# A second Strassen level for product 4 of batches 3 to 6 with its sums on GpSimd, and x transposed in blocks of two tokens of one head

## The chip, the cores and the metric

The kernel runs on one core of a Trainium2 chip. A core has five engines with a queue each: TensorE (PE; its weight loads are listed apart, as PEld), VectorE (DVE), ScalarE (ACT), GpSimd (POOL) and SyncE (SP, which here only issues transfers). Each queue is worked in order; an instruction that waits for another engine holds back everything behind it on its own engine. The metric is the device time of one execution in microseconds. The kernel before took 201.92 us (median of three runs, 201.89 to 202.7).

## The reference

Per batch (8) and head (8), x has 512 tokens of 64 values and the state 32 rows of 64.

```python
a  = softmax(x @ state.T / 8);   xread = a @ state     # 512 x 64 per head
a2 = softmax(state @ x.T / 8);   sread = a2 @ x        #  32 x 64 per head
attn = concat([xread, sread], axis=2)                  # 544 rows per batch, 512 wide
h = attn @ w_in                                        # 512 -> 2048
out = (0.5 * h * (1 + erf(h / sqrt(2)))) @ w_out       # 2048 -> 512
```

The inputs and the output (4352 x 512) are float32; the kernel computes in bfloat16 with float32 sums.

## The kernel before, in words

**First matrix product.** For the 512 read rows of a batch, w_in is multiplied into the state first: `p_mm` forms P = state · w_in, so that h = a · P. `scores` forms x · state^T and its exponential `e`; `norm` (DVE) makes `a`; a DMA transpose (`atr_dma`) makes `AT`. `M(i)` (`mm1`) is one 128-row block of h^T, two matmuls of 512 columns (L506) with a gelu on ACT that writes `g` (L513). There are 16 such blocks per batch.

**Second matrix product.** g^T · w_out (512 x 2048 by 2048 x 512) is done by Strassen's scheme in Winograd's form: seven products of quadrants, named "1" to "7". Products 1, 2 and 4 take a quadrant of g as it is; 5, 6, 7 and 3 take sums of quadrants that DVE forms (`g_sum`, tile `gsum`). The right sides are quadrants of w_out or differences of them (`w_diff`, tiles `ws`). A product is 16 matmuls of 256 columns (L647) into one bank; `X(b, name)` runs it and hands the bank to ACT (`snap`, a copy to SBUF) or to DVE (an add into the output tile `oh`). `c4`, the copy of product 4, is used by `c21`, the add into the left half of the second output tile, after product 7 of the same batch.

**The second level.** Product 2 of batches 2 to 7 is already split again into seven small products of four matmuls with 128 columns each (`sub_mm`, L727). `sub_sums` makes the four left sums on DVE (`gsub`). `sub_a` runs 2, 1, 4, 5 into the four quarters of the bank, and ACT copies the bank to `qa` (L741). `sub_b` adds 6 and 3 and restarts quarter 0 with 7 in that same bank, ACT copies it to `qb` (L749), and three adds on DVE make `c2`. The pools `cpool` give one buffer per tag.

**Order.** The order is written out by hand. A batch b has eight slots p = 0 to 7. Each holds two blocks `M` of batch b; slots 0 to 5 hold products 1, 6, 5, 7 and 3 of batch b-1, the scores of batch b+1 (slot 1), its norm (slots 2 and 3) and its `p_mm` (slot 5, `p_all`). Slot 5 ends with `sub_a`, slot 6 with `sub_b`, slot 7 with product 4 of batch b. The last batch's slots 0 to 4 interleave the rows of sread (`read_out_slot`).

**x.** POOL issues the load of x (with a cast) into `xb`, where a partition holds four tokens of every head. `rearr` (POOL) makes a copy `x4` in which the blocks of 128 columns pair two heads, and `xtr_dma` (SP) transposes these blocks to `xT` by DMA; batch 1 is transposed on PE (`xtr`, L271). `rearr_ones` (POOL) makes `xo`, the copy with a column of ones for sread. `sbd` holds the transposed states, block-diagonal for the two heads of a block; `state_prep` (L160, L166) fills it with one PE transpose per batch. `hold_for` is a one-element POOL copy that delays the next load until a given gelu.

The change and the prediction's steps touch `state_prep`, `xtr`, `xtr_dma`, `scores`, `rearr`, `w_subs`, `sub_sums`, `sub_a`, `sub_b` and the order of the loop.

Of the kernel before, what the change touches and what calls it, by code (L numbers as in the profile page):

```python
# [17 lines left out]
def kernel(  # L18
# [8 lines left out]
    nc = tc.nc  # L27
# [41 lines left out]
    sbd = persist.tile([128, B, HC, 2 * NS], BF16, name="sbd")  # L69
# [7 lines left out]
    sb0 = persist.tile([128, 2, 2, 2, NS], BF16, name="sb0")  # L77
    hold = persist.tile([128, 1], BF16, name="hold")
    spare = persist.tile([128, 1], FP32, name="spare")
    warm = persist.tile([128, 512], BF16, name="warm")  # L80
    xos = [persist.tile([128, SJ, HC, 132], BF16, name=f"xo_{i}") for i in range(2)]
    x4s = [persist.tile([128, SJ, HC, 128], BF16, name=f"x4_{i}") for i in range(2)]
# [12 lines left out]
    nc.gpsimd.memset(sbd, 0.0)  # L95
# [38 lines left out]
    def load_rest():  # L134
        load_w_out(4, 6)
        load_w_out(6, 8)
        load_w_in(1024, 1536)
        load_w_out(8, 12)
        load_w_in(1536, 2048)
        load_st(2, 3)  # L140
        load_x(2)
        load_w_out(12, 16)
        load_x(3)

# [10 lines left out]

    def state_prep(b0, b1, pool=ps_f, tag="f"):
        n = b1 - b0
        ps = pool.tile([128, n, HC, NS], BF16, name="st_ps", tag=tag)
        for b in range(b0, b1):
            nc.tensor.transpose(  # L160
                ps[:, b - b0, :, :].rearrange("p c n -> p (c n)"),
                st_bf[:, b, :, :].rearrange("q t d -> q (t d)"),
                ident,
            )
        for t in range(2):
            nc.vector.tensor_copy(  # L166
                out=sbd[64 * t:64 * t + 64, b0:b1, :, 32 * t:32 * t + 32].rearrange(
                    "d b c n -> d (b c) n"
                ),
                in_=ps[64 * t:64 * t + 64, :, :, :].rearrange("d b c n -> d (b c) n"),  # L170
            )
# [23 lines left out]
    def state0_p(ps):  # L195
        for t in range(2):
            h = slice(64 * t, 64 * t + 64)
            nc.scalar.copy(out=sbd[h, 0, :, 32 * t:32 * t + 32], in_=ps[h, 2, :, :])
# [7 lines left out]
    def begin(b):  # L206
        A = Att()
        atts[b] = A
        A.x4 = x4s[b % 2]
        A.xo = xos[b % 2]  # L210
        if b > 0:
            A.xT = att.tile([128, SJ, HC, 128], BF16, name="xT", tag="xT")
# [7 lines left out]

    def rearr(b, ts=(0, 1)):
        A = atts[b]
        src = xbs[b].rearrange("p (t c) (j d) -> p t c j d", t=2, d=D)
        for t in ts:
            nc.gpsimd.tensor_copy(  # L225
                out=A.x4[:, :, :, 64 * t:64 * t + 64].rearrange("p j c d -> p c j d"),
                in_=src[:, t],
            )
# [35 lines left out]
    def xtr(b, cs):  # L264
        A = atts[b]
        xv = xbs[b].rearrange("p (t c) (j d) -> p j c t d", t=2, d=D)
        ps = ps_f.tile([128, len(cs), SJ, 128], BF16, name="xT_ps", tag="f")
        for i, c in enumerate(cs):
            for j in range(SJ):
                for t in range(2):  # L270
                    nc.tensor.transpose(ps[64 * t:64 * t + 64, i, j, :], xv[:, j, c, t, :], ident)  # L271
        nc.vector.tensor_copy(
            out=A.xT[:, :, cs[0]:cs[0] + len(cs), :].rearrange("p j c n -> p c j n"), in_=ps
        )

    def xtr_dma(b):
        A = atts[b]
        nc.sync.dma_start_transpose(
            out=A.xT.rearrange("p j c n -> p (j c) n"),
            in_=A.x4.rearrange("p j c n -> p (j c n)"),  # L280
# [44 lines left out]
    def scores(b, half):  # L325
# [4 lines left out]
        for ci in range(2):  # L330
            c = 2 * half + ci
            for j in range(SJ):
                nc.tensor.matmul(  # L333
                    pt[:, j, :, ci, :],
                    lhsT=A.xT[:, j, c, :],
                    rhs=sbd[:, b, c, :],
                    start=True,
                    stop=True,
                )
# [95 lines left out]
    def p_mm(b, f, tiles):  # L435
# [3 lines left out]
        for c in range(HC):  # L439
            for t in range(2):  # L440
                nc.tensor.matmul(  # L441
                    ps[t][32 * c:32 * c + 32, :],
                    lhsT=sbd[64 * t:64 * t + 64, b, c, 32 * t:32 * t + 32],
# [36 lines left out]
    def pmat00(h):  # L480
# [3 lines left out]
        for c in range(HC):  # L484
            for t in range(2):
                nc.tensor.matmul(
                    ps[t][32 * c:32 * c + 32, :],
                    lhsT=sbd[64 * t:64 * t + 64, 0, c, 32 * t:32 * t + 32],
# [868 lines left out]
```

## Time and profile before

| what | us |
|---|---|
| median of three runs | 201.92 |
| the profiled execution | 202.25 |
| its span (first to last instruction) | 200.3 |
| PE busy | 193.9 (97%) |
| DVE busy | 155.1 (77%) |
| ACT busy | 145.6 (73%) |
| POOL busy | 48.1 (24%) |

The profiled execution is 1.95 us longer than its span: that lies ahead of the first and behind the last instruction shown. The granted TensorE clock is full in all 40 slices. A busy share is an average over the whole span; whether an engine is late in one place is read from the timeline there. In the timeline a line holds the start, the time from start to the end of the last instruction of the group, the engine, line, operation, tiles and count, and in brackets idle time and what ended it. Matmuls follow each other faster than each ends (one of 512 columns every 0.22 us, though each is listed with 0.38), so the time that a group costs PE is the distance to the start of the next group.

### The profile page before, as it was taken

How to read it: one execution, taken by the hardware profiler on the slowest of the kernel's cores; microseconds unless marked ns; L12 is line 12 of the kernel's file. 1: busy time of each engine (PE TensorE's matmuls, PEld its weight loads, DVE VectorE, ACT ScalarE, POOL GpSimd, SP SyncE). 2: the span in 40 equal slices, each digit the busy share in tenths (PEclk: the TensorE clock that was granted, in tenths of full speed). 3: DMA queues.
4: the chain of work that ended last, by engine and by line, in shares of the span. 5: the costliest groups of instructions: out<-in, count | busy, mean ns of one | idle time of the engine just before them, and what ended most of it. 6: DMA issues, size and time to landing. Idle time of an engine off the chain costs nothing.

```text
span 200.3 us, 5055 instructions
## 1 busy us (share of the span) xinstructions
PE 193.9 (97%) x2102; PEld 134.3 (67%) x2107; DVE 155.1 (77%) x279; ACT 145.6 (73%) x264; POOL 48.1 (24%) x65
## 2 busy tenths in 40 slices
PE   7899999999999999999999999999999999999993
PEld 2533544465767777767777787677776888878893
DVE  2963796969989769975997798849966897984863
ACT  3785577699896799569966997599948778775120
POOL 8972504543403444040504300030000000000000
PEclk9999999999999999999999999999999999999999
DMA  5999999976494959680797025420024010030044
GB/s 192 197 174 202 206 199 201 183 136 142 84 149 77 241 65 164 141 214 0 77 188 209 5 67 95 138 75 27 28 107 106 0 55 0 7 153 0 18 146 157
DMA packets 40567, 23.16 MB, mean 116 GB/s; under 512 B 21856, under 2 KB 39136, under 8 KB 40544
## 3 DMA queue, kind: packets, MB, share of 16 engines
q0 software_dynamic: 13984, 8.10, 29.9%
q1 hardware_dynamic: 25728, 14.22, 27.5%
q10 hardware_dynamic: 832, 0.52, 0.8%
q8 instruction: 16, 0.26, 0.5%
q14 instruction: 7, 0.06, 0.1%
HBM read 17.30 MB, written 8.91 MB: 131 GB/s over the span
## 4 chain that ended last, share of the span: by engine, by line
PE 86%; DMA 5%; POOL 4%; ACT 2%; issue 0%; DVE 0%; POOLq 0%
PE xp L647 36%; PE hp L506 26%; DMA xb<-in_x_dram 5%; PE xp L727 5%; PE op L548 3%; PE sp L866 3%; PE rp L932 3%; POOL w_in_bf L105 2%; PE op L532 2%; PE xp L773 2%; PE pt L333 2%; ACT P L1002 1%; PE p_ps L441 1%; PE sr L962 1%; POOL sbd L95 1%; POOL w_out_bf L113 1%
## 5 line engine op out<-in xcount | busy, mean ns | idle before, releaser
L513 ACT ACTIVATE g<-hp 128x512 bf16<-128x512 f32 x124 | 67.1, 614 | 17.0 <-PE hp L506 16.8
L506 PE MATMUL hp<-AT,P 128*128 128x512 bf16 x248 | 62.2, 379 | 0.0
L647 PEld LDWEIGHTS <-gsum 128*128 128x128 bf16 x416 | 40.4, 98 | 8.9 <-issue 0.4
L647 PE MATMUL xp<-ws,gsum 128*128 128x256 bf16 x320 | 38.2, 273 | 0.0
L506 PEld LDWEIGHTS <-P 128*128 128x128 bf16 x248 | 23.0, 98 | 19.4 <-ACT P L452 0.7
L647 PEld LDWEIGHTS <-g 128*128 128x128 bf16 x240 | 23.3, 98 | 4.8
L637 DVE TENSOR_TENSOR gsum<-g 128x2048 bf16<-128x2048 bf16 x14 | 17.0, 1218 | 0.6 <-ACT g L513 0.6
L225 POOL COPY x<-xb 128x1024 bf16<-128x1024 bf16 x12 | 12.2, 1044 | 18.5 <-DMA xb<-in_x_dram 18.5
L235 POOL COPY xo<-xb 128x1024 bf16<-128x1024 bf16 x12 | 12.2, 1043 | 14.1 <-PE sr L962 13.9
L647 PE MATMUL xp<-w_out_bf,g 128*128 128x256 bf16 x128 | 15.3, 273 | 0.0
L647 PE MATMUL xp<-ws,g 128*128 128x256 bf16 x112 | 13.4, 273 | 0.0
L1016 POOL COPY hold<-g 128x1 bf16<-128x1 bf16 x7 | 2.3, 334 | 42.9 <-ACT g L513 42.9
L666 DVE TENSOR_TENSOR c<-qb 128x256 f32<-128x256 f32 x6 | 2.6, 425 | 12.7 <-ACT qb L749 12.7
L548 PE MATMUL op<-w_out_bf,g 128*128 128x512 bf16 x44 | 11.0, 380 | 0.5 <-issue 0.3
L647 PE MATMUL xp<-w_out_bf,gsum 128*128 128x256 bf16 x96 | 11.5, 273 | 0.0
L666 DVE TENSOR_TENSOR oh<-xp,c 128x512 f32<-128x512 f32 x14 | 9.6, 686 | 2.4 <-PE xp L647 2.0
L1002 DVE CAST P<-p_ps 128x512 bf16<-128x512 f32 x15 | 9.4, 683 | 2.4 <-PE p_ps L441 2.4
L356 DVE TENSOR_TENSOR a<-e,ics 128x512 bf16<-128x512 bf16 x14 | 10.5, 750 | 0.5
L353 DVE TENSOR_REDUCE cs<-e 128x16 f32<-128x512 bf16 x14 | 9.5, 678 | 0.9 <-ACT e L340 0.9
L513 ACT ACT_TABLE_LOAD x7 | 9.0, 1283 | 0.1
L441 PE MATMUL p_ps<-w_in_bf,sbd 64*32 64x512 bf16 x248 | 9.0, 380 | 0.0
L637 DVE TENSOR_TENSOR gsum<-gsum,g 128x2048 bf16<-128x2048 bf16 x7 | 8.6, 1225 | 0.2
(155 smaller groups left out, 308.9 us busy)
## 6 DMA issues: line engine op xcount, KB each, us to landing
out_dram<-oh SPq DMA_DIRECT2D x15, 256.0 KB, 3.3
xb<-in_x_dram POOLq DMA_DIRECT2D x7, 512.0 KB, 7.1
out_dram<-oh SPq DMA_DIRECT2D x6, 512.0 KB, 3.1
w_in_bf<-in_moe_w_in_dram POOLq DMA_DIRECT2D x6, 256.0 KB, 11.7
out_dram<-osb SPq DMA_DIRECT2D x5, 256.0 KB, 3.0
w_out_bf<-in_moe_w_out_dram POOLq DMA_DIRECT2D x4, 256.0 KB, 7.8
w_out_bf<-in_moe_w_out_dram POOLq DMA_DIRECT2D x2, 512.0 KB, 13.3
x0f<-in_x_dram SPq DMA_DIRECT2D x3, 256.0 KB, 3.8
```

What stands on the lines that cost most here:

```text
L225: nc.gpsimd.tensor_copy(out=A.x4[:, :, :, 64 * t:64 * t + 64].rearrange("p j c d -> p c j d"), in_=src[:, t],)
L235: eng.tensor_copy(out=A.xo[:, :, :, 2 + 64 * t:66 + 64 * t].rearrange("p j c d -> p c j d"), in_=src[:, t],)
L356: nc.vector.tensor_tensor(out=A.a[:, :, hs].rearrange("p g (c n) -> p g c n", n=NS), in0=e4, in1=ics[:, :, :].to_broadcast((128, G, 2, NS) ...
L441: nc.tensor.matmul(ps[t][32 * c:32 * c + 32, :], lhsT=sbd[64 * t:64 * t + 64, b, c, 32 * t:32 * t + 32], rhs=w_in_bf[64 * t:64 * t + 64, c ...
L506: nc.tensor.matmul(hp, lhsT=Ps[b][:, t, m * 128:(m + 1) * 128], rhs=atts[b].AT[:, :, t, :], start=(t == 0), stop=(t == 1),)
L513: nc.scalar.activation(out=gs[b][:, m, :], in_=hp, func=AF.Gelu)
L548: nc.tensor.matmul(ops[b, j], lhsT=gs[b][:, m, j * 128:(j + 1) * 128], rhs=w_out_bf[:, m, :], start=(m == 0), stop=(m == MC - 1),)
L637: nc.vector.tensor_tensor(out=got[name], in0=x, in1=y, op=op)
L647: nc.tensor.matmul(ps[:, j - js[0], :], lhsT=lhs[:, m, 128 * j:128 * j + 128], rhs=rhs[:, m, :], start=(first and j == js[0] and m == 0), ...
L666: nc.vector.tensor_tensor(out=out, in0=x, in1=y, op=ALU.add)
L727: nc.tensor.matmul(xs[b, 0][:, at, :], lhsT=lhs[:, m, :], rhs=rhs[:, m, :], start=(start and m == 0), stop=(m == MH // 2 - 1), skip_group_ ...
L1002: copy(out=Ps[b][:, t, f * 512:(f + 1) * 512], in_=ps[t])
```

## The change

Product 4 of batches 3 to 6 is split as product 2 is: `sub_sums(b, "4")` in slot 5, `sub_a(b, "4")` in slot 7 in place of product 4, `sub_b(b, "4")` in slot 0 of the next batch, after its two blocks `M`. The left sums are on DVE, the three closing adds on POOL. The differences of the right side (`w_subs("4", ...)`, four DVE instructions) are formed once, in slot 3 of batch 3. Both units use the same two buffers, `qa` and `qb`. Copies that had other homes move: product 5's copy to the buffer of `c2`, the sums of the sread part to `late4` and other tiles.

`rearr` and `x4` are gone. The DMA transpose reads `xb` directly, in blocks of 128 columns that hold two tokens of one head. `sbd` becomes block-diagonal for two copies of the same head's state (twice the size, its second half cleared later on POOL); `state_twice` writes the state doubled side by side, on POOL (DVE for batch 1), and `state_prep` takes two transposes per batch. `scores` has as many matmuls as before, one per head and pair of tokens.

```diff
+    def state_twice(b0, b1, eng):
+        eng.tensor_copy(
+            out=st2[:, b0 % 4:b0 % 4 + b1 - b0].rearrange("q b t u d -> q (b t) u d"),
+            in_=st_bf[:, b0:b1].rearrange("q b t d -> q (b t) d")[:, :, None, :].broadcast_to(
+                [128, 2 * (b1 - b0), 2, D]
+            ),
+        )
...
+        for b in range(n):
+            for t in range(2):
+                nc.tensor.transpose(
+                    ps[:, b, HC * t:HC * t + HC, :].rearrange("p c n -> p (c n)"),
+                    st2[:, (b0 + b) % 4, t].rearrange("q u d -> q (u d)"),
+                    ident,
+                )
...
-    def rearr(b, ts=(0, 1)):
-        A = atts[b]
-        src = xbs[b].rearrange("p (t c) (j d) -> p t c j d", t=2, d=D)
-        for t in ts:
-            nc.gpsimd.tensor_copy(
-                out=A.x4[:, :, :, 64 * t:64 * t + 64].rearrange("p j c d -> p c j d"),
-                in_=src[:, t],
-            )
...
+        for i, h in enumerate(hs):
+            for q in range(SJ // 2):
+                nc.tensor.transpose(ps[:, i, q, :], xbs[b][:, h, 128 * q:128 * q + 128], ident)
...
         nc.sync.dma_start_transpose(
-            out=A.xT.rearrange("p j c n -> p (j c) n"),
-            in_=A.x4.rearrange("p j c n -> p (j c n)"),
+            out=A.xT.rearrange("p h q n -> p (h q) n"),
+            in_=xbs[b].rearrange("p h d -> p (h d)"),
         )
...
-    def sub_a(b):
-        xs[b, 0] = otile([128, 4, QN], "xp", 0)
+    def sub_a(b, unit):
+        ps = xs[b, BANK[unit]] = otile([128, 4, QN], "xp", BANK[unit])
         for at, name in enumerate("2145"):
-            sub_mm(b, name, at, at == 0)
-        xs[b, "qa"] = cpool.tile([128, 4, QN], FP32, name="qa", tag="s5")
-        nc.scalar.copy(out=xs[b, "qa"], in_=xs[b, 0])
+            sub_mm(b, unit, name, at, at == 0)
+        xs[b, "qa"] = cpool.tile([128, 4, QN], FP32, name="qa", tag="qa")
+        nc.scalar.copy(out=xs[b, "qa"], in_=ps)
...
+    def sub_b(b, unit):
+        sub_mm(b, unit, "6", 1)
+        sub_mm(b, unit, "3", 3)
+        sub_mm(b, unit, "7", 0, True)
         qa = xs[b, "qa"]
-        qb = cpool.tile([128, 4, QN], FP32, name="qb", tag="u")
-        nc.scalar.copy(out=qb, in_=xs[b, 0])
...
+        qb = cpool.tile([128, 4, QN], FP32, name="qb", tag="qb")
+        nc.scalar.copy(out=qb, in_=xs[b, BANK[unit]])
+        name = "c" + unit
+        c = xs[b, name] = c_tile(name)
...
+        for out, x, y in (
+            (c[:, 0], qb[:, 1:2, :].broadcast_to(wide), qb[:, 0:4:3, :]),
+            (c[:, 1], c[:, 0, 0:1, :].broadcast_to(wide), qa[:, 2:4, :]),
+            (c[:, 0, 0, :], qa[:, 1, :], qa[:, 0, :]),
+        ):
+            (nc.vector if unit == "2" else nc.gpsimd).tensor_tensor(out=out, in0=x, in1=y, op=ALU.add)
...
             if p < 5 and nb < B:
                 if p == 0:
+                    if b > 3:
+                        sub_b(b - 1, "4")
                     g_sum(b - 1, "56")
...
                 if p == 3:
-                    sub_sums(b)
+                    sub_sums(b, "2")
+                    if b == 3:
+                        w_subs("4", range(4))
...
-                sub_a(b)
+                sub_a(b, "2")
+                if b > 2:
+                    sub_sums(b, "4")
...
             if p == 6:
-                sub_b(b)
+                if b == 2:
+                    state_prep(4, B)
+                sub_b(b, "2")
             if p == 7:
                 if nb == B - 1:
                     srts(reads)
-                X(b, "4")
+                if b > 2:
+                    sub_a(b, "4")
+                else:
+                    X(b, "4")
```

In `read_out_slot(0)` the line `sub_b(c, "4")` stands in the same place, after the blocks `M`.

## The prediction

> **What bounds the kernel now.** I read the page first: the busy shares, then the chain that ended last.
>
> ```profile
> span 200.3 us, 5055 instructions
> PE 193.9 (97%) x2102; PEld 134.3 (67%) x2107; DVE 155.1 (77%) x279; ACT 145.6 (73%) x264; POOL 48.1 (24%) x65
> ...
> PE 86%; DMA 5%; POOL 4%; ACT 2%; issue 0%; DVE 0%; POOLq 0%
> ```
>
> TensorE is busy 97% and makes 86% of the chain; nearly all the rest is the first 19 us, in which DMAs are awaited. From 20 us on PE is almost never idle, so a microsecond of matmul taken away is a microsecond gained, and any wait that PE meets is lost for good. So I went to the timeline at the place where the change puts its new matmuls, the end of a batch. This is batch 5 (the others look the same), engine by engine, with PE first.
>
> ```profile
> 130.37 0.61 PE L727 MATMUL xp<-w_out_bf,g 128*128 128x128 bf16 x8
> ...
> 131.26 1.03 PE L506 MATMUL hp<-AT,P 128*128 128x512 bf16 x4
> 132.12 0.39 PE L727 MATMUL xp<-q_w,gsub 128*128 128x128 bf16 x4
> ...
> 132.79 1.03 PE L506 MATMUL hp<-AT,P 128*128 128x512 bf16 x4
> 133.65 1.91 PE L647 MATMUL xp<-ws,g 128*128 128x256 bf16 x16
> 135.40 1.03 PE L506 MATMUL hp<-AT,P 128*128 128x512 bf16 x4
> ```
>
> By the starts: the first half of product 2 (16 matmuls) takes 131.26 - 130.37 = 0.89, two blocks M 0.86, the second half (12 matmuls) 132.79 - 132.12 = 0.67, product 4 takes 135.40 - 133.65 = 1.75.
>
> ```profile
> 131.46 0.58 ACT L741 COPY qa<-xp 128x512 f32<-128x512 f32 x1 [0.16 <-PE xp L727]
> 131.94 1.08 ACT L1307 CAST P<-p_ps 128x512 bf16<-128x512 f32 x2
> 132.89 1.12 ACT L513 ACTIVATE g<-hp 128x512 bf16<-128x512 f32 x2
> 133.86 0.63 ACT L749 COPY qb<-xp 128x512 f32<-128x512 f32 x1
> 134.32 1.16 ACT L513 ACTIVATE g<-hp 128x512 bf16<-128x512 f32 x2
> 135.60 0.58 ACT L670 COPY c<-xp 128x512 f32<-128x512 f32 x1
> ```
>
> ACT runs here without a gap and late: the second half of product 2 is through at 132.79, its copy `qb` only starts at 133.86, behind two casts and two gelus. The table of busy time for 132.12 to 138.17 gives ACT 5.91 of 6.05 us.
>
> ```profile
> 129.86 1.89 DVE L1002 CAST P<-p_ps 128x512 bf16<-128x512 f32 x3 [0.36 <-PE p_ps L441]
> 134.52 0.42 DVE L666 TENSOR_TENSOR c<-qb 128x256 f32<-128x256 f32 x1 [2.78 <-ACT qb L749]
> 134.98 0.42 DVE L666 TENSOR_TENSOR c<-c,qa 128x256 f32<-128x256 f32 x1
> 135.44 0.29 DVE L666 TENSOR_TENSOR c<-qa 128x128 f32<-128x128 f32 x1
> ```
>
> DVE's three closing adds of product 2 wait for that late copy and end at 135.73. The last of them is the last reader of the buffer `qa`.
>
> **The change, part by part.**
>
> *Matmuls.* Four times product 4 (1.75) becomes 0.89 + 0.67 = 1.56. PE gains 4 x 0.19 = 0.76 us.
>
> *The new wait.* The second half of unit 4 adds into the bank of the first half, so its first matmul waits for the copy of that bank to `qa`. That copy must wait for the buffer: `qa` has one buffer, and unit 2 of the same batch holds it until its third add. Before, that buffer was next wanted in slot 2 of the next batch, by product 5's copy; now it is wanted two slots after it was filled. Worked out for batch 5: the first half of unit 4 starts where product 4 did, 133.65, and ends at 134.54; the blocks M last until 135.40; there PE meets the second half. The third add ends at 135.73, the copy starts 0.04 later (such handovers take 0.02 to 0.05 in the chain), takes 0.58, and after another 0.04 PE goes on at 136.39. Wait 0.99. The same lines of batches 3, 4 and 6 have the third add end at 93.60, 114.88 and 156.97 and the M after product 4 start at 93.27, 114.55 and 156.75: waits of 0.99, 0.99 and 0.88. Sum 3.85.
>
> Three things could move that. The new left sums on DVE (four of 0.42, one each 0.34 to 0.45, 1.55 in all by the same sums of unit 2) fit into the 2.78 of idle time ahead of the adds in odd batches; in even ones the idle time is 1.00 (batch 4) and 1.86 (batch 6), and in batch 4 it grows by 0.86, since one small DVE instruction there took 1.15 instead of 0.29 beside a POOL copy that is removed. So the adds are not later. Without the wait for DVE at all, ACT alone would reach `qa` when its gelus are through, 135.30 to 135.48, so PE would go on at 135.9 to 136.1 and still wait 0.5 to 0.7. That is the lower bound. Queued behind the copy on ACT are the gelus of slot 0 and then `qb` of unit 4; the exponential's table load follows and would end at about 0.7 after its old time, while PE's scores are 0.8 later: no second wait. I take 3.85, with bounds 2.0 to 4.3 (the upper one if the sums end 0.1 late each time).
>
> *The differences for unit 4's right side*, once, in slot 3 of batch 3, on DVE, four instructions like these sums:
>
> ```profile
> 86.03 0.42 DVE L721 TENSOR_TENSOR gsub<-g,gsub 128x512 bf16<-128x512 bf16 x1
> 86.68 0.69 DVE L666 TENSOR_TENSOR oh<-xp,u 128x512 f32<-128x512 f32 x1 [0.24 <-PE xp L647]
> 87.73 1.89 DVE L1002 CAST P<-p_ps 128x512 bf16<-128x512 f32 x3 [0.36 <-PE p_ps L441]
> ```
>
> They come between the first two lines: starts at 86.37, 86.82, 87.16, 87.50, so the add of product 3 starts at 87.84, 1.16 later, and frees its bank at 88.53. The fourth pair of P blocks on PE wants that bank at 87.84 (24 of 32 matmuls, at 0.035, after 87.00). It starts at 88.57, and product 2 after it at 88.85 instead of 88.23: 0.62. Bounds 0 and 0.9.
>
> *State and x on PE.* The transposes of the state go from 7 to 14, at 0.056 each (five took 0.28). The extra one of batch 1 lies in the 0.23 in which PE waits for x of batch 1. Six remain: 0.34. Batch 1's own transposes shrink from 32 (1.08) to 16 (0.90), but the first scores now need both halves of xT, whose second copy on DVE ends at 21.3, where those scores start now: no gain. Bounds 0.1 and 0.6.
>
> *POOL and SP.* Removed: 12 copies of 1.04. No wait of PE, ACT or DVE in the chain names them, because the x blocks are ready long before their scores; the transposes start earlier and nothing follows from that. Added: three adds per batch. The trace has no POOL add; by its copies (1024 elements in 1.04) one of 256 costs 0.26 at least, and four times that, 1.04, if both inputs and four bytes count in full: 0.65 to 2.6 us for three. They start at about 96 in batch 3, and `c21` reads them at 105: hidden by 6 us in either case. Queued behind them on POOL is the load of x two batches ahead, which is 2.6 later at most and not wanted for 20 us. The doubled state for batches 3 on waits behind the state's load, which lands about 2 us ahead of its transposes at 48.3.
>
> A rule that speaks against this part: the Trainium skill (GPSIMD Engine Reference, section 4.1 Engine selection) sends elementwise arithmetic to VectorE, as a two-input operation takes about twice as long on GpSimd; its table of 3.1 has 4497 ns for 2048 elements, from which I estimate about 1.4 us for the three adds. No run here shows it yet. By the rule the move costs time, by the 6 us of cover nothing, and the sum would be the same.
>
> *POOL against DVE.* While a POOL copy ran at 96.07 to 98.09, a DVE sum of 1024 elements took 1.96 instead of 0.68. If the three adds block DVE likewise, it loses up to 1.3 per batch in slots 0 and 1; there it has the 0.8 by which PE is later, and the removed copies did the same harm. I take 0; bounds -0.2 and +0.5 per batch.
>
> **Sum.** -0.76 + 3.85 + 0.62 + 0.34 = +4.05. The profiled execution, 202.25, would become 206.3; the median 201.92 is 0.33 lower, so I forecast 206.0 us (span about 204.3), slower by 2%.
>
> **The rivals.**
>
> 1. *ACT alone sets the wait.* The third add comes early enough, and PE waits 0.5 to 0.7 per batch; with the differences of batch 3 half hidden: 201.92 - 0.76 + 2.4 + 0.3 + 0.34 = 204.2 (203.5 to 205.1). For it: ACT is the engine that is late. Against: in all four batches the add ends 0.2 after ACT's gelus.
>
> 2. *The adds on POOL cost.* They block DVE by 0.5 per batch net, so that sums reach PE late in slots 1 to 3: 206.0 + 2 = 208.0 (206.9 to 208.5). For it: DVE runs from 92.4 to 107 with hardly a gap. Against: POOL loses more copies than it gets adds.
>
> 3. *Not slower.* The copy to `qa` is done before PE is through with the blocks M, so the wait is nil. This takes a third add that ends 1.0 us earlier and, on ACT, two gelus fewer ahead. Then 201.92 - 0.76 + 0.34 = 201.5, or 202.1 with the differences of batch 3. It decides from waits below 0.1 per batch. Against: both engines would have to be early in all four batches.
>
> **How the numbers follow.** Forecast 0.62, rival 1 0.15, rival 2 0.13, rival 3 0.10. The forecast's own range is 205.2 to 206.8. A change of 0.5%, 1.0 us, is about what a measurement here can tell from none. Slower by more: 0.62 + 0.15 + 0.13 = 0.90; rival 3 splits into 0.06 within it and 0.04 faster. The range takes in rivals 1 and 2 but for their ends: 203.6 to 208.0.
>
> **What would show it.** In the changed profile, ACT's copies to `qa` should number ten, and in batches 3 to 6 the second one of a batch should be followed by a PE gap of about 1.0 us ahead of L732, charged to ACT; that copy should start right after DVE's third add. The 28 small matmuls should cost 1.56. In batch 3 the P blocks should show a gap of about 0.6 charged to DVE's add. Were the gaps 0.5, rival 1 holds; were there new gaps ahead of L650 charged to DVE, rival 2; were there none, rival 3, and I would be wrong about the buffer.

## The result and the profile after

The changed kernel takes 206.96 us (median of four runs, 206.33 to 208.14) against 201.9 before: ratio 1.0249, interval 1.0222 to 1.0275. The forecast was 206.0 with 203.6 to 208.0. The profiled execution is the longest of the four, 208.14 us with a span of 206.4. Single executions that lay far above the others of their kernel (287.4 us of the kernel before, 402.9 and 226.2 of two kernels below) are left out of all times here. The page:

```profile
span 206.4 us, 5188 instructions
...
PE 195.3 (95%) x2146; PEld 134.6 (65%) x2146; DVE 162.4 (79%) x302; ACT 148.0 (72%) x268; POOL 50.2 (24%) x69
...
PE 69%; DMA 12%; DVE 6%; ACT 5%; POOL 5%; issue 1%; ACTq 0%; POOLq 0%
```

TensorE's share of the chain that ended last falls from 86% to 69%. DVE and ACT together, 2% before, now make 11%: the chain leaves TensorE at the new waits and comes back. The DMA share, 5% before and 12% now, is the startup: here the chain runs along two transfers of weights until 36 us, where before it was on TensorE from 22 us on. That is another path more than another time; what it is worth stands in the account below. The waits of PE, with the total, the number and the longest:

```profile
PE xp L732 <- ACT qa L746: 3.6, 4, 0.9
...
PE p_ps L440 <- DVE oh L669: 0.7, 1, 0.7
```

Four waits for `qa`, one for the add of batch 3: what the prediction named, and no other of that size behind the startup. Batch 5 again, PE, ACT and DVE in the timeline:

```profile
137.25 0.61 PE L732 MATMUL xp<-ws,g 128*128 128x128 bf16 x8
...
138.14 1.03 PE L505 MATMUL hp<-AT,P 128*128 128x512 bf16 x4
140.11 0.38 PE L732 MATMUL xp<-q_w,gsub 128*128 128x128 bf16 x4 [0.94 <-ACT qa L746]
...
140.77 1.91 PE L650 MATMUL xp<-w_out_bf,g 128*128 128x256 bf16 x16
```

```profile
137.95 1.16 ACT L512 ACTIVATE g<-hp 128x512 bf16<-128x512 f32 x2
139.47 0.59 ACT L746 COPY qa<-xp 128x512 f32<-128x512 f32 x1 [0.36 <-DVE c L764]
```

```profile
138.15 0.43 DVE L764 TENSOR_TENSOR c<-qb 128x256 f32<-128x256 f32 x1 [1.14 <-ACT qb L754]
138.61 0.43 DVE L764 TENSOR_TENSOR c<-c,qa 128x256 f32<-128x256 f32 x1
139.07 0.29 DVE L764 TENSOR_TENSOR c<-qa 128x128 f32<-128x128 f32 x1
```

Read them as one story. The first half of unit 4 is through at 138.14. ACT's gelus end at 139.11, but the copy to `qa` waits 0.36 more, until DVE's third add of unit 2 (ended 139.36) has let go of the buffer. The copy ends at 140.06, PE goes on at 140.11. The bracket says 0.94, but the price is larger: the blocks M of 138.14 take 0.86 to the next start when nothing waits, and here they take 140.11 - 138.14 = 1.97. PE lost 1.11. The listed end of a matmul lies 0.17 behind the point at which the next could have started, so every gap after a group of wide matmuls costs 0.17 more than its bracket. By the same reading the four waits cost 1.10, 1.10, 1.11 and 1.00, 4.31 in all.

The P blocks of batch 3, on PE, and on DVE the last of the four new differences and the add that follows it:

```profile
87.97 0.84 PE L440 MATMUL p_ps<-w_in_bf,sbd 64*32 64x512 bf16 x24
89.53 0.41 PE L440 MATMUL p_ps<-w_in_bf,sbd 64*32 64x512 bf16 x8 [0.72 <-DVE oh L669]
89.87 0.62 PE L732 MATMUL xp<-w_out_bf,g 128*128 128x128 bf16 x8
```

```profile
88.46 0.42 DVE L598 TENSOR_TENSOR q_w<-ws,q_w 128x512 bf16<-128x512 bf16 x1
88.79 0.68 DVE L669 TENSOR_TENSOR oh<-xp,u 128x512 f32<-128x512 f32 x1
```

The add ends at 89.47 and PE goes on at 89.53. From 87.97 to 89.87 is 1.90; before it was 1.23. That is 0.67 lost.

**The account.** The start of the last DVE instruction, L669's last add, moved from 197.32 to 202.50, by 5.18. On PE's path that is: waits for `qa` +4.31, batch 3 +0.67, four products 4 as two halves -0.76 (0.89 or 0.90 and 0.66 or 0.67 instead of 1.75), and +0.96 that is there already when the scores of batch 4 begin, in slot 1 of batch 3 (75.99 instead of 75.03). Their sum is 5.18. That it fits to the hundredth is chance: PE also loses 0.04 to 0.06 in each of the four batches ahead of unit 2's second half (0.92 from 134.80 to 135.72, before 0.86), and about as much is gained in the read-out, where two waits of 0.08 and 0.09 are gone. Of the +0.96, 0.74 is there at 42 us, when the scores of batch 2 begin; that moment differs from execution to execution (42.72 here, 41.4 to 43.2 in the kernels below, 41.98 before) and is no property of the change. The other 0.22 arises between 42 and 75 us, where the state is transposed.

Behind that last add the old kernel needs 2.69 us to the end of the span, the new one 3.57. No step of the prediction had that. The transfers of the last microseconds, in the changed kernel:

```profile
q8 instruction: 1, 0.02, 0.8%
q14 instruction: 2, 0.02, 0.7%
...
out_dram<-oh SPq DMA_DIRECT2D x2, 256.0 KB, 2.8
out_dram<-oh ACTq DMA_DIRECT2D x1, 128.0 KB, 3.0
out_dram<-oh SPq DMA_DIRECT2D x1, 64.0 KB, 2.9
out_dram<-oh ACTq DMA_DIRECT2D x1, 64.0 KB, 2.6
```

Ahead stand the two queues that bring instructions, with packets, MB and share, then the issues of the last 6.5 us, with the time from issue to landing at the end of a line. Before, the same transfers landed after 2.1, 2.1, 2.0 and 1.7, and in that window there was one instruction packet (queue 14) where there are now three. Two questions were thus open for the runs: whether the five waits are made by what the prediction said, and what the tail is.

### The profile page after: what moved, and what is told of

Read it like the earlier page. It is cut to its first block, busy times and chain, and to the rows that moved or that the text cites. A ratio compares the mean times of both kernels' runs of the same rounds, so it can differ in the third digit from the quotient of the medians.

```text
span 206.4 us, 5188 instructions
## 1 busy us (share of the span) xinstructions
PE 195.3 (95%) x2146; PEld 134.6 (65%) x2146; DVE 162.4 (79%) x302; ACT 148.0 (72%) x268; POOL 50.2 (24%) x69
## 4 chain that ended last, share of the span: by engine, by line
PE 69%; DMA 12%; DVE 6%; ACT 5%; POOL 5%; issue 1%; ACTq 0%; POOLq 0%
PE xp L650 31%; PE hp L505 19%; DMA w_out_bf<-in_moe_w_out_dram 12%; PE xp L732 7%; PE sp L879 3%; PE rp L951 3%; DVE c L764 2%; POOL w_in_bf L106 2%; PE xp L783 2%; ACT g L512 2%; PE pt L332 1%; DVE ws L575 1%; ACT qa L746 1%; PE sr L981 1%; POOL w_out_bf L114 1%
## 5 line engine op out<-in xcount | busy, mean ns | idle before, releaser
L650 PEld LDWEIGHTS <-gsum 128*128 128x128 bf16 x416 | 40.4, 98 | 8.9 <-issue 0.4
L650 PE MATMUL xp<-ws,gsum 128*128 128x256 bf16 x320 | 38.2, 273 | 0.0
L669 DVE TENSOR_TENSOR oh<-xp,c 128x512 f32<-128x512 f32 (+1 forms) x22 | 14.2, 664 | 8.2 <-PE xp L650 5.8
L650 PEld LDWEIGHTS <-g 128*128 128x128 bf16 x176 | 16.9, 98 | 2.7
L650 PE MATMUL xp<-w_out_bf,g 128*128 128x256 bf16 x128 | 15.3, 273 | 0.0
L732 PE MATMUL xp<-q_w,gsub 128*128 128x128 bf16 x120 | 11.6, 219 | 3.6 <-ACT qa L746 3.6
L732 PEld LDWEIGHTS <-gsub 128*128 128x128 bf16 x160 | 10.1, 97 | 6.4 <-issue 5.3
L764 POOL TENSOR_TENSOR c<-qb 128x256 f32<-128x256 f32 x4 | 3.7, 923 | 40.0 <-ACT qb L754 40.0
L547 PE MATMUL op<-w_out_bf,g 128*128 128x512 bf16 x48 | 11.8, 380 | 0.1
L650 PE MATMUL xp<-w_out_bf,gsum 128*128 128x256 bf16 x96 | 11.5, 273 | 0.0
L1035 POOL COPY hold<-g 128x1 bf16<-128x1 bf16 x7 | 3.4, 481 | 33.0 <-ACT g L512 33.0
L440 PE MATMUL p_ps<-w_in_bf,sbd 64*32 64x512 bf16 x248 | 9.9, 381 | 0.8 <-DVE oh L669 0.7
L355 DVE TENSOR_TENSOR a<-e,ics 128x512 bf16<-128x512 bf16 x14 | 9.7, 692 | 0.5
L673 ACT COPY c<-xp 128x512 f32<-128x512 f32 x10 | 6.0, 596 | 5.1 <-PE xp L650 4.5
```

The source lines that it names most:

```text
L355: nc.vector.tensor_tensor(out=A.a[:, :, hs].rearrange("p g (c n) -> p g c n", n=NS), in0=e4, in1=ics[:, :, :].to_broadcast((128, G, 2, NS) ...
L440: nc.tensor.matmul(ps[t][32 * c:32 * c + 32, :], lhsT=sbd[64 * t:64 * t + 64, b, HC * t + c, 32 * t:32 * t + 32], rhs=w_in_bf[64 * t:64 * ...
L547: nc.tensor.matmul(ops[b, j], lhsT=gs[b][:, m, j * 128:(j + 1) * 128], rhs=w_out_bf[:, m, :], start=(m == 0), stop=(m == MC - 1),)
L650: nc.tensor.matmul(ps[:, j - js[0], :], lhsT=lhs[:, m, 128 * j:128 * j + 128], rhs=rhs[:, m, :], start=(first and j == js[0] and m == 0), ...
L669: nc.vector.tensor_tensor(out=out, in0=x, in1=y, op=ALU.add)
L732: nc.tensor.matmul(xs[b, BANK[unit]][:, at, :], lhsT=lhs[:, m, :], rhs=rhs[:, m, :], start=(start and m == 0), stop=(m == MH // 2 - 1), sk ...
```

## The experiments

The kernel before ran beside each group, at 201.95 to 202.18 us. Unless said otherwise an edit starts from the changed kernel.

### One buffer more

```diff
-        xs[b, "qa"] = cpool.tile([128, 4, QN], FP32, name="qa", tag="qa")
+        xs[b, "qa"] = cpool.tile([128, 4, QN], FP32, name="qa", tag="qa" if unit == "2" else "qa4")
...
-    st2 = persist.tile([128, B - 4, 2, 2, D], BF16, name="st2")
+    st2 = cpool.tile([128, B - 4, 2, 2, D], BF16, name="st2", tag="qa4")
```

> The changed kernel, but product 4's first half is copied to a buffer of its own (the room comes from the doubled state, which is dead by then). The prediction's theory, that the copy waits for the buffer until DVE's third add: the copy starts when ACT's two gelus are through, 0.4 us earlier per batch, so the four waits of PE ahead of the second half (3.6 us in the changed kernel's profile) fall to about 2.1 and the time from 206.96 to about 205.4. Rival, ACT alone sets the wait: the waits stay at 3.6 and the time within 0.4 of 207.0. If the buffer were all of it, the waits would go to 0 and the time to 203.3.

Measured: ratio 1.0134 (1.0057 to 1.0210), three executions at 204.5 to 205.7, the middle one 205.1. In PE's timeline and in ACT's:

```profile
138.23 0.38 PE L732 MATMUL xp<-q_w,gsub 128*128 128x128 bf16 x4 [0.44 <-ACT qa L746]
```

```profile
136.54 1.16 ACT L512 ACTIVATE g<-hp 128x512 bf16<-128x512 f32 x2
137.51 0.67 ACT L746 COPY qa<-xp 128x512 f32<-128x512 f32 x1
```

The copy now follows the gelus directly. The waits are 0.47, 0.44, 0.44 and 0.33, 1.7 in all where 2.1 was expected, so about half of each was the buffer and the other half is ACT's queue. Rival 1's mechanism is the floor under the forecast's: it needs the buffer out of the way to be seen.

### The second half later

`sub_b(b - 1, "4")` goes behind product 1 instead of ahead of it, in slot 0 and in the read-out's slot 0.

```diff
-                    if b > 3:
-                        sub_b(b - 1, "4")
...
                     X(b - 1, "1657"[p])
+                    if p == 0 and b > 3:
+                        sub_b(b - 1, "4")
```

> The changed kernel, but the second half of product 4 runs after product 1 in slot 0 instead of before it; nothing is added or left out. If the loss is only that PE reaches the second half too early, 1.75 us of matmuls more cover the wait of 0.94: no wait of PE ahead of L732, 206.96 - 3.6 = 203.3 us. Rival, the wait only moves: the copy to qb and behind it the exponential's table load come 1.75 us later on ACT, the exponentials of slot 1 are late and PE waits 0.5 or more per batch for their banks: 205 us or above.

Measured: 205.29, ratio 1.0149 (1.0075 to 1.0222). The waits ahead of L732 are gone, and in batch 4 to 5 another has come:

```profile
122.33 0.27 PE L423 MATMUL srT<-ident,srm 128*128 128x128 bf16 x2 [1.10 <-ACT g L512]
```

```profile
117.38 0.59 ACT L754 COPY qb<-xp 128x512 f32<-128x512 f32 x1 [0.64 <-PE xp L732]
117.99 1.28 ACT L339 ACT_TABLE_LOAD   x1
```

ACT is in order. Now it waits 0.64 for the later second half to copy `qb`, and the exponential's table load, the exponentials and the gelus of slot 1 stand behind that copy; PE runs into the late gelus. In the read-out there is one more wait, 0.80. The rival of this run holds: of the four waits only a part is saved, as a half that moves takes its ACT copy along.

### The parts alone

First the x part (doubled state, x^T of one head, no `rearr`) with product 4 whole; then the second level with the old x part.

```diff
-                    if b > 3:
-                        sub_b(b - 1, "4")
...
-                    if b == 3:
-                        w_subs("4", range(4))
...
-                if b > 2:
-                    sub_sums(b, "4")
...
-                if b > 2:
-                    sub_a(b, "4")
-                else:
-                    X(b, "4")
+                X(b, "4")
```

This is the first of the two; `sub_b(c, "4")` in the read-out goes too. The second is the kernel before with the edits of the change that concern product 4 and the buffers.

> The changed kernel with product 4 left whole in all batches, so only the x blocks, the doubled state and the moved buffers remain of the change. The prediction has +0.34 for it (six more transposes of the state): 202.2 us. In the profile after, the first scores of batch 2 come 0.7 us later than before; if that belongs to this part and not to the scatter of the first DMAs, 202.8 to 203.2. If taking POOL's copies away helped DVE, below 201.9.

> The changed kernel with the x part undone (pairing copy of x, blocks of two heads, state and its preparation as before), so that only the second level of product 4 with its adds on GpSimd remains. The prediction has -0.76 + 3.85 + 0.62 = +3.7 for it: 205.6 us; by the steps read off the profile after (0.87, 0.96, 0.97, 0.85 per batch net, and 0.75 in batch 3) +4.4: 206.3. Rival, the adds on GpSimd together with the pairing copies on the same queue hold DVE up: above 207, with new waits of PE for DVE's sums ahead of the products of slots 1 to 3.

Measured: the x part alone 202.25, ratio 1.0013 (0.9984 to 1.0042), last DVE instruction at 197.37, 0.05 later than before. POOL's busy time falls from 48.1 to 40.3 us and nothing comes of it. The transposes show in a stretch, not in that total, as this execution's startup was 0.30 shorter: from the scores of batch 1 to those of batch 2, and from these to those of batch 4, TensorE takes 20.82 + 33.26 here and 20.75 + 33.05 before, 0.28 more; the medians differ by 0.25, which the interval does not tell from nothing. The second level alone 207.49, ratio 1.0247 (1.0183 to 1.0312): gaps of 0.94, 0.94, 0.94, 0.83 and 0.72 as in the changed kernel, last DVE instruction at 201.00, 3.68 later. All of the loss is in the second level. The time is 1.2 us above the 206.3 expected, in the region of this run's rival, but the rival's waits of PE for DVE's sums are not there. In the profiled execution, the fastest of the four, 1.0 of the loss is the tail (3.7 instead of 2.7); why the others took up to 1.1 more is not shown.

### The adds on DVE

```diff
-            (nc.vector if unit == "2" else nc.gpsimd).tensor_tensor(out=out, in0=x, in1=y, op=ALU.add)
+            nc.vector.tensor_tensor(out=out, in0=x, in1=y, op=ALU.add)
```

> The changed kernel with the three closing adds of unit 4 on VectorE, as unit 2 has them. The prediction's rival two (the adds cost time because GpSimd takes 2.2 us where VectorE takes 1.14) would have this faster, 205.5 to 206.4, with the waits of unit 2's second half unchanged. Theory (GpSimd's adds end long before c4 is read, in slot 3): nothing is gained, 207.0 to 208.0, the waits ahead of the second half stay at 0.9 to 1.0 us, VectorE is 4.6 us busier.

Measured: 217.5, ratio 1.0768 (1.0730 to 1.0805). Both theories miss it by some 10 us. PE's waits, and DVE at the end of batch 5:

```profile
PE xp L650 <- DVE oh L669: 5.9, 3, 2.0
PE xp L732 <- ACT qa L746: 3.6, 4, 0.9
PE sp L879 <- DVE srt L900: 1.9, 1, 1.9
```

```profile
147.97 0.42 DVE L764 TENSOR_TENSOR c<-qb 128x256 f32<-128x256 f32 x1 [2.29 <-ACT qb L754]
...
149.10 1.22 DVE L640 TENSOR_TENSOR gsum<-g 128x2048 bf16<-128x2048 bf16 x1
```

DVE stands 2.29 us still, waiting for unit 4's `qb`, and the sums for products 5 and 6, which could have been formed in that time, come after, and so does the add that frees product 1's bank on PE. The three waits ahead of L650 and the one ahead of L879 cost, with 0.17 each, 8.4 us; after the first of them the granted TensorE clock fell to 0.50 for 3.4 us besides, which is 1.7 us more. POOL has nothing behind its adds that is wanted soon, so there the same wait is free. In the changed kernel, batch 5:

```profile
141.69 0.73 POOL L764 TENSOR_TENSOR c<-qb 128x256 f32<-128x256 f32 x1 [6.09 <-ACT qb L754]
142.50 0.73 POOL L764 TENSOR_TENSOR c<-c,qa 128x256 f32<-128x256 f32 x1
143.31 0.46 POOL L764 TENSOR_TENSOR c<-qa 128x128 f32<-128x128 f32 x1
```

One add takes 1.7 times as long as on DVE (0.73 against 0.43), and the three 2.1 us. The rule of the Trainium skill (GPSIMD Engine Reference, section 4.1 Engine selection) sends elementwise arithmetic to VectorE and gives a two-input operation on GpSimd about twice the time. The factor of 1.7 measured here is near that, and yet following the rule cost some 10 us: what counted was not the duration but what is queued behind a wait.

### The subtractions on GpSimd

The four subtractions of unit 4's weight leave DVE in batch 3 for POOL in slot 6 of batch 2.

```diff
                 hold_for(b, 12)
                 load_x(5)
+                w_subs("4", range(4), nc.gpsimd)
...
-                    if b == 3:
-                        w_subs("4", range(4))
```

> The changed kernel, with the four subtractions of the weight of unit 4 taken off VectorE in slot 3 of batch 3 and given to GpSimd in slot 6 of batch 2. Theory (they delay the add that frees bank 2): the wait of 0.72 us ahead of p_ps in batch 3 goes to the 0.1 us or less of the other batches, the chain is 0.6 us shorter from there on, 206.96 becomes about 206.3. Rival (bank 2 is late for another reason, such as the six extra transposes or the adds of unit 4): the wait stays at 0.72 and the time at 207.0.

Measured: 211.09, ratio 1.0450 (1.0418 to 1.0482). The wait of 0.72 in batch 3 is gone, as the theory said, and 4 us are lost elsewhere. POOL and DVE at that time, and then PE:

```profile
72.15 1.17 POOL L598 TENSOR_TENSOR q_w<-ws 128x512 bf16<-128x512 bf16 x1
73.40 1.22 POOL L598 TENSOR_TENSOR q_w<-ws,q_w 128x512 bf16<-128x512 bf16 x1
```

```profile
71.68 1.93 DVE L764 TENSOR_TENSOR c<-qb 128x256 f32<-128x256 f32 x1 [0.29 <-ACT qb L754]
73.65 1.26 DVE L764 TENSOR_TENSOR c<-c,qa 128x256 f32<-128x256 f32 x1
74.94 1.12 DVE L764 TENSOR_TENSOR c<-qa 128x128 f32<-128x128 f32 x1
75.99 2.17 DVE L640 TENSOR_TENSOR gsum<-g 128x2048 bf16<-128x2048 bf16 x1
```

```profile
80.19 2.50 PE L650 MATMUL xp<-ws,gsum 128*128 128x256 bf16 x16 [3.08 <-DVE oh L669]
```

The DVE instructions take 1.93, 1.26, 1.12 and 2.17 where they take 0.42, 0.42, 0.29 and 1.22 without company; each ends 0.1 to 0.3 after a POOL instruction, or 1.1 for the long sum, about its own time. By these ends they take turns, whole instruction by whole instruction. PE's wait explains 3.25 of the loss. For the rest, the table of stretches of PE's first microseconds after it (the columns behind POOL's are the granted clock, the DMA share and GB/s):

```profile
81.00:82.00 1.00, 1.00 (x9) 0.79 (x7) 0.96 (x3) 0.00 (x0) 0.00 (x0) 0.67 1.33 168
82.00:83.00 1.00, 1.00 (x6) 0.52 (x5) 0.92 (x2) 0.22 (x1) 0.00 (x0) 0.50 1.15 129
83.00:84.00 1.00, 1.00 (x4) 0.36 (x3) 0.00 (x0) 0.78 (x2) 0.00 (x0) 0.50 1.32 242
```

About 1.2 us after PE starts again its clock is halved, for 3.4 us: 0.33 + 0.50 + 0.50 + 0.38 of a microsecond, 1.7 us more, by the clock of each stretch (0.62 in the one after these). 3.25 + 1.7 - 0.67 is 4.3; the medians differ by 4.1.

The exclusion itself is a known rule. The Trainium skill (SBUF — State Buffer, section Who interferes with whom) has just this: a DVE instruction with two inputs from SBUF contends with a GpSimd instruction that reads SBUF, and the ports that they share are an exclusive lock. The runs agree. In the changed kernel DVE's adds from PSUM ran beside the closing adds on POOL at their usual 0.69 (142.72, beside 142.50); where DVE had a sum of two tiles in SBUF at the same time, the POOL adds were held up (1.51 instead of 0.73 in batch 6, 1.01 instead of 0.46 in batch 3), and DVE's two sums beside the adds of batch 3 took 1.54 together instead of 1.28.

### The mends together

Second level without the x part, own buffer for unit 4, the subtractions on POOL as above, and the second half in slot 1 behind its blocks M, where ACT has done its exponentials.

```diff
+                if p == 1 and b > 3:
+                    sub_b(b - 1, "4")
                 if p < 4:
                     X(b - 1, "1657"[p])
```

> The second level for unit 4 without the x part, with the three mends together: qa of unit 4 in a buffer of its own, the weight's subtractions on GpSimd in batch 2, and the second half of unit 4 moved from slot 0 to slot 1, behind that slot's first-layer pair, so that the copy of qb does not stand ahead of the exponentials on ScalarE. Theory (what was lost lies in these waits alone): no wait above 0.2 us charged to qa, qb or oh, and what is left is product 4 itself, 0.76 us less over four batches: the last VectorE instruction starts 0.8 us earlier than before; with a tail of 2.7 us 201.1, with the tail of 3.6 us that the changed kernel showed 202.0. Rival (the adds on GpSimd or the extra ScalarE copy cost by themselves wherever the half stands): a wait of 0.4 to 1.1 us per batch ahead of some other TensorE instruction, 203.5 to 205.5.

Measured: 207.24, ratio 1.0282 (1.0240 to 1.0324). No wait for `qa` is left, so the new place works; but POOL's subtractions cost here what they cost above (one wait of 3.42, this time with the clock at 1.00 after it), and in the read-out PE comes 0.77 too early for the sums `srx`. The next kernel has the subtractions on DVE in slot 6 of batch 2, where DVE was idle, and product 1 ahead of the state products in the read-out:

```diff
             if p == 6:
+                if b == 2:
+                    w_subs("4", range(4))
                 sub_b(b, "2")
...
+            X(c, "1")
             SR("3", 0)
             SR("4", 0)
-            X(c, "1")
```

> The second level without the x part and with the mends, but with the weight's four subtractions back on VectorE, in slot 6 of batch 2 ahead of unit 2's closing adds, where VectorE stood idle for 1.86 us, and with product 1 of batch 6 ahead of the first state products in the read-out's slot 0. Theory (GpSimd's subtractions held VectorE up by a shared resource, and nothing else was left but the wait for srx): no TensorE wait above 0.2 us after 30 us, four times 0.19 us gained on TensorE, the last VectorE instruction 0.2 to 0.8 us earlier than before at 196.5 to 197.1; the time 201.1 to 201.7 if the stretch behind it is 2.7 us and 202.0 to 202.6 if an instruction block lands in it. Rival (moving the second half to slot 1 has a price of its own, on ScalarE or by TensorE's banks): a new wait of 0.3 us or more in every batch, 203 or more.

Measured: 202.91, ratio 1.0037 (1.0024 to 1.0051). Up to the read-out there is no wait above 0.2; from the scores of slot 1 in one batch to those in the next PE takes 20.67 where it took 20.85 (batch 5 to 6), but 21.26 where it took 21.28 (batch 4 to 5). But the new order made its own wait, two of 0.23 and

```profile
160.88 0.61 PE L881 MATMUL sp<-XSR,srw 128*128 128x128 bf16 x8 [1.09 <-DVE srt L902]
```

because the output add of product 1 now stands on DVE ahead of the state's sum. So the old order again, and instead `srx` ahead of unit 2's closing adds:

```diff
+        if between is not None:
+            between()
         name = "c" + unit
         c = xs[b, name] = c_tile(name)
...
-                sub_b(b, "2")
+                sub_b(b, "2", (lambda: (srts(reads), sr_x("34"))) if nb == B - 1 else None)
```

> As the mended kernel with the subtractions on VectorE, but the read-out's slot 0 in its old order, and at the end of batch 6 the transposes of the last state reads and the two sums srx issued ahead of unit 2's closing adds on VectorE. Theory (the 1.1 us wait for srt was made by putting product 1 first, and with srx ready 1 us earlier nothing waits): no TensorE wait above 0.2 us after 30 us, the last VectorE instruction 0.5 to 0.9 us earlier than before (196.4 to 196.8), the time 201.2 to 202.1, at or just below the kernel before. Rival (the read-out of batch 7 needs the half of unit 4 out of its way for another reason): a wait of 0.3 to 1.1 us stays in the read-out's slots 0 to 2, 202.2 to 203.2.

Measured: 202.47, ratio 1.0026 (1.0013 to 1.0039). One wait of 0.17 is left behind the startup. In the profiled execution the last DVE instruction starts at 197.55: 0.54 late at 42 us, 0.31 gained after. That is what the second level is worth on PE when its waits are gone, less than half of the 0.76 that its matmuls give, and still the kernel is 0.5 us slower than before. In the profiled execution 1.0 is lost in the tail, 3.7 us; but it is the longest of twelve (203.37), so what makes the median slower is not shown.

### The tail

The instruction blocks on queue 8 are packets of 16 KB (0.28 MB in 17 packets, by the page). The last of them arrived at 202.1 in the changed kernel. To move it, the warming matmuls of the startup were cut into pieces of 128 columns: the same columns, 76 more rows in PE's stream.

```diff
-            w = 128 * min(n, 4)
+            w = 128
...
-            n -= 4
+            n -= 1
```

> The changed kernel with the same columns of warming matmuls in the startup, but each of 128 columns instead of up to 512: 38 more TensorE instructions with 38 more weight loads, no more work. In the changed kernel and in the second level alone an instruction block arrived at 202.0 and 200.0 us, among the last output transfers, and the stretch behind the last VectorE instruction was 3.6 us; in the kernels in which that block came after the end or not at all it was 2.7. Theory (the block's arrival slows the last transfers): the boundary of the block moves about 3.5 us earlier, away from the last transfers, the stretch falls to 2.7 and the time to about 206.1. Rival (the tail is long for another reason): the stretch stays at 3.6, the time at 207.0.

Measured: 206.24, ratio 1.0214 (1.0194 to 1.0234), against 1.0249 (1.0222 to 1.0275); the intervals just overlap, so that the time is shorter is likely rather than certain. In the profile the block came at 198.3, so it belongs to PE's stream, and the tail is 2.7. The last 8 us:

```profile
q8 instruction: 1, 0.02, 0.7%
...
out_dram<-oh SPq DMA_DIRECT2D x2, 256.0 KB, 2.2
out_dram<-osb SPq DMA_DIRECT2D x1, 256.0 KB, 3.8
out_dram<-oh ACTq DMA_DIRECT2D x1, 128.0 KB, 2.1
out_dram<-oh SPq DMA_DIRECT2D x1, 64.0 KB, 2.0
out_dram<-oh ACTq DMA_DIRECT2D x1, 64.0 KB, 1.7
```

The last transfers are back at 2.0 and 1.7, and the transfer from `osb`, which the block now meets, takes 3.8 where it takes 3.0 in the kernel before. The delay went with the block; the last block of queue 14, the other instruction queue, stood 0.8 ahead of the last add in both kernels. All fourteen profiles side by side: the start of the last DVE instruction, the start of the last block on each instruction queue against it, the landing times of the two last transfers (64 KB each, SP's and ACT's), and the stretch from the end of that instruction to the end of the span.

| kernel | last DVE | block, queue 8 | block, queue 14 | 64 KB | stretch |
|---|---|---|---|---|---|
| before | 197.32 | 10.5 earlier | 2.5 earlier | 2.0, 1.7 | 2.7 |
| x part alone | 197.37 | 9.4 earlier | 1.7 later | 2.0, 1.8 | 2.7 |
| adds on DVE | 212.96 | 14.1 earlier | 2.4 earlier | 2.0, 1.8 | 2.7 |
| own buffer | 200.36 | 4.1 later | 2.4 earlier | 2.0, 1.7 | 2.7 |
| half later | 199.25 | 4.7 later | 0.8 earlier | 2.0, 1.7 | 2.7 |
| finer warming | 201.79 | 3.5 earlier | 0.8 earlier | 2.0, 1.7 | 2.7 |
| changed | 202.50 | 0.4 earlier | 0.8 earlier | 2.9, 2.6 | 3.6 |
| subtractions on POOL | 206.35 | 0.8 earlier | 0.8 earlier | 2.9, 2.3 | 3.4 |
| second level alone | 201.00 | 0.9 earlier | 1.1 later | 3.0, 2.7 | 3.7 |
| mends together | 200.86 | 1.0 earlier | 1.0 later | 3.0, 2.7 | 3.7 |
| subtractions on DVE | 197.99 | 1.0 earlier | 1.7 later | 2.2, 1.9 | 2.9 |
| srx early | 197.55 | 1.1 earlier | 1.5 later | 3.0, 2.7 | 3.7 |
| ... with all warming cut | 199.59 | 3.5 earlier | 1.7 later | 2.0, 1.7 | 2.7 |
| ... with the first burst cut | 196.89 | 3.9 earlier | 1.3 later | 2.0, 2.5 | 3.5 |

A block of queue 8 within 1.1 us of the last add goes with a stretch of 2.9 to 3.7; otherwise it is 2.7, but for the last row. For the changed kernel the pair with the finer warming speaks for the block as the cause, with one profile of each. In three other rows (the second level alone, the mends together, `srx` early) a block of queue 14 stands 1.0 to 1.5 behind the last add as well, and there it is open which of the two counts: the subtractions on DVE have the queue 8 block in the same place without the other, and only 0.2 more. The two last rows were attempts to bring the mended kernels below the one before: the subtractions on DVE with all warming cut (the edit above), and `srx` early with only the first burst cut, by a parameter of `keep_warm`:

```diff
-    keep_warm(28)
+    keep_warm(28, 1)
```

> The kernel of the previous run with its warming matmuls cut into pieces of 128 columns, which adds 76 instructions to TensorE's stream and nothing to its work. Theory (a block of TensorE's instructions that arrives among the last output transfers lengthens them by 0.8 us): the block arrives 3 to 4 us earlier and the stretch behind the last VectorE instruction is 2.7 us, the time 201.1 to 201.7, 0.5 to 0.9 less than without if that one's stretch is 3.6. Rival: same stretch in both, times within 0.3 us of each other.

> The kernel of the previous run with only the first warming burst cut into pieces of 128 columns, 42 more rows in TensorE's stream and no more work. In the previous run a block arrived at 196.25 us and the stretch from the last VectorE instruction to the end was 3.6 us of a time of 202.47. Theory (the block costs 0.8 us there): it arrives 1.3 to 1.8 us earlier, ahead of the four last transfers, the stretch is 2.7 to 2.9 us, the last VectorE instruction starts 0.2 to 0.5 us earlier than before and the time is 201.6 to 202.0, at or 0.2 us below the kernel before. Rival (a block that moves slows whatever it then meets, as the transposed transfer of AT at 51 us met one when 76 instructions were added): a TensorE wait of 1 us or more appears elsewhere and the time stays above 202.3.

Measured: 204.26, ratio 1.0104 (1.0086 to 1.0122), and seven executions at 202.3 to 202.7, ratio 1.0023 (1.0009 to 1.0036). The first has its stretch of 2.7, and is slower all the same: PE waits 1.37 at 51.75 for the transposed transfer to `AT`, while a block arrives at 49.5, 2.3 us earlier than without the cut; whether the block makes that wait was not tried. The second has the earliest last DVE instruction of all, 196.89, no wait on PE above 0.16 behind the startup, its block at 193.0, out of the way, and yet a stretch of 3.5:

```profile
out_dram<-oh SPq DMA_DIRECT2D x1, 64.0 KB, 2.0
out_dram<-oh ACTq DMA_DIRECT2D x1, 64.0 KB, 2.5
```

Only the last transfer is slow now. The block of queue 14 arrives at 198.2, 1.3 us after the start of the last add; in the kernels where it comes 1.7 after it and no block of queue 8 is near, the x part alone and the one with all warming cut, the stretch is 2.7. So this may be the cause, but no run moved that block by itself. I had not expected it, and it stays open. None of the kernels tried is faster than the one before.

## Why the prediction was right, and where it was off

**Forecast 206.0, measured 206.96, the mechanism as stated.** By the number alone it could have been otherwise: 206.96 lies just above the 205.2 to 206.8 that the prediction gave the forecast by itself, and at the lower end of rival 2's 206.9 to 208.5. The waits decide for the forecast's mechanism; what lifts the number is above all the tail, which was in no step. Step by step:

- *Matmuls*, -0.76: right. The first half takes 0.89 or 0.90, the second 0.66 or 0.67, product 4 took 1.75.
- *The new wait*, 3.85: the cause is shown. The copy to `qa` ends its wait at DVE's third add in all four batches (0.36 each), and a second buffer halves PE's wait. The size was too small: 4.31. The third add ended 0.36 after PE was through with the blocks M, 0.33 had been worked out; the copy started 0.11 after the add instead of 0.04; that makes 1.11 instead of 0.99 in a batch.
- *The lower bound*, ACT alone, 0.5 to 0.7 per batch: with the buffer taken away the brackets are 0.33 to 0.47, with 0.17 added 0.50 to 0.64. Right.
- "*No second wait*" behind the copy: right for the changed kernel, where no wait follows. It depends on the place: with the half moved behind product 1 the table load behind `qb` came late and cost 1.10.
- *The differences of unit 4's right side*, 0.62: measured 0.67, and the wait vanished both when they went to POOL and when they went to an idle place on DVE.
- *State and x on PE*, +0.34: about right, 0.28 in the x part alone by its stretches, 0.22 of it between 42 and 75 us in the changed kernel too. The startup differs by more than that from one execution to the next.
- *POOL and SP*, nothing: right, no wait of PE names them. The three adds take 2.1 us in batches 4 and 5, 2.6 in batch 3 and 2.9 in batch 6, where DVE's sums held them up; the last is above the bounds of 0.65 to 2.6.
- *POOL against DVE*, 0 with -0.2 to +0.5: right, and by luck of the place. DVE's two sums beside the adds of batch 3 lose 0.3, and no wait of PE follows. The subtractions on POOL show what the exclusion costs where DVE's instructions have two inputs from SBUF and PE is near: 3.25 us for four instructions, before the clock.
- *The sum* left out the end of the program: about 0.9 us in the tail of the profiled execution, the largest single error. In numbers: +4.05 predicted; 4.31 + 0.67 - 0.76 + 0.28 = 4.50 on PE and 0.88 in the tail make 5.38; the medians differ by 5.06, so some 0.3 is scatter of the start or of the tail; which, a single profile does not show.

**The rivals.** Rival 1 fell: with ACT alone the time is 205.1, not 206.96; its mechanism is what remains once the buffer is free. Rival 2 fell: there is no gap ahead of L650 charged to DVE. Its opposite is shown, as the adds on DVE cost 10 us. Rival 3 fell: no wait was below 0.8.

## What to carry to other kernels

A buffer that is held to the last read of a chain across three engines (here PE, ACT, DVE) can become a wait when a second user comes soon after the first: count when the last reader ends, not when the writer is through. Work that has to wait went better here on the engine whose queue behind it was empty, though it took 1.7 times as long there; and before putting two-input work on GpSimd look for two-input work on VectorE at the same time. A bracket of idle time is not the price: take the distance of starts with and without the wait.

## What the runs showed of the hardware

- Two-input instructions on DVE and POOL with their inputs in SBUF exclude each other: adds of 0.42 and 0.29 on DVE took 1.93 and 1.12 beside POOL subtractions of 1.2, and PE lost 3.25 us; in the changed kernel a POOL add of 0.73 took 1.51 beside a sum on DVE. Beside DVE adds with one input from PSUM, both kept their time (0.69 and 0.73).
- After a wait of 3.1 us, and in another kernel after the first of three waits of 2.0, TensorE's granted clock went to 0.50 for 3.4 us, beginning 1.2 and 1.3 us after it took up work again: 1.7 us lost behind the wait. After the two later waits of 2.0 and after a wait of 3.4 in a third kernel it stayed at 1.00, and the waits of 0.9 never brought it about. What decides was not tried.
- An instruction block of 16 KB that arrives among output transfers can lengthen them by 0.8 to 0.9 us (64 KB: 2.0 to 2.9, and 1.7 to 2.6). When it was moved by adding 76 instructions to PE's stream, the delay moved with it, to a transfer of 256 KB (3.0 to 3.8). One such block 1.0 us ahead of the last add, in the kernel with the subtractions on DVE, cost only 0.2. So the length of a program may decide some 0.4% of its time (206.96 and 206.24) at a place that has nothing to do with the edit. What the other instruction queue's blocks do was not settled.
